# First routing search counted in PSUM ring banks, and the second expert's gather asked one block earlier

## The chip, the cores and the metric

The kernel is one program on one core of a Trainium2 chip. Its five engines run their own queues: TensorE (PE) with its weight loads (PEld), VectorE (DVE), ScalarE (ACT), GpSimd (POOL) and SyncE (SP), which mostly issues DMA transfers; POOL issues transfers too. The metric is the device time of one execution in microseconds, lower is better.

## The reference

Attention over 4 batches, 8 heads, 576 positions of 64 gives a matrix `x` of 2304 tokens by 512. Then a mixture of 8 experts and a feed-forward layer follow. What matters here is how tokens get their expert:

```
def _moe_ref(x, w_gate, w1, w2):
    ...
    cap = N // E                       # 2304 // 8 = 288
    logits = x @ w_gate
    order = np.argsort(-logits.flatten())
    assigned = -np.ones(N); counts = np.zeros(E)
    for idx in order:
        tok, e = idx // E, idx % E
        if assigned[tok] >= 0 or counts[e] >= cap:
            continue
        assigned[tok] = e
        counts[e] += 1
    for e in range(E):
        mask = assigned == e
        h = np.maximum(x[mask] @ w1[e], 0.0)
        out[mask] = h @ w2[e]

def _moe2_ref(x, w_in, w_out):
    h = x @ w_in
    g = np.maximum(h, 0.0) + np.log1p(np.exp(-np.abs(h)))
    return g @ w_out
```

## The kernel before

**Attention** fills the first 196 us, writes the tokens to a DRAM array `xs` and leaves the gate's logits `L` on chip, 18 columns of 128 tokens by 8 experts. Then `FFN.run` handles the experts one after the other in the order in which they fill up.

**Routing.** `Router.phase` finds one expert: the one that is full first, and its 288 tokens. It looks for the logit at which an expert's count reaches its capacity, by `search`: 4 steps over the high bits and 5 over the low ones, each a 32-way division. In a step DVE compares all keys with 31 thresholds, in two halves of 9 columns (line 601, into `rcmp`); PE counts per expert (two matmuls of line 610 with the capacities, 18 of line 614); DVE reduces the counts to the number of thresholds passed (line 617); PE spreads this number over the partitions (line 619); and DVE subtracts it from the keys (line 607) while the next step's comparisons have already read it. `r.key`, `r.lo`, the counts `r.pc`, the number `r.pn`, the tokens' positions `r.pos` and the index sums `r.pi` are all slices of one PSUM bank, tile `rt`. Between the steps DVE also converts pieces of the weight `w_in` (lines 527, 529, 532 on tiles `ce`), taken from the generator `load_in`.

After the search, DVE sums up who belongs to the expert (lines 654 to 689), PE turns this into positions (lines 692, 693), DVE compares the positions with a row of 128 numbers (line 711, three rounds of two, tiles `roa`), and PE sums the token numbers up (line 717). The result is `ridx` (line 725), by which `gather` fetches the tokens with three indirect DMAs from POOL (line 935, tiles `xr`). `Router.close` prepares the logits for the next expert. `route` strings the phases together as a generator: each `yield` gives a kind, the number of ticks to wait before the next piece, and a cost.

**One expert.** `xpose` transposes the gathered tokens on PE (line 949) and splits them into halves `xgh`, `xgl`. `H1` and `Y` are the expert's two layers, in 8 blocks. Then come 16 blocks `i` of the feed-forward layer: `H2(i + 2)` is a column block of `w_in` (12 matmuls, into a bank of the tag `ring`, which has 3 of them), `G` is the softplus on ACT and DVE (lines 995 to 1008, the last a copy of the remainder on POOL), and `O(i)` is the row block of `w_out` (6 matmuls of 512 columns into `acc`). In the first expert, `split_out` splits w_out's block into halves on ACT and POOL (line 917) and stores them to DRAM array `wh` (line 918, SP), and `load_out` loads them back for the next expert (line 925, POOL, 512 KB each). `tails` splits the last pieces of w_in (lines 858, 861).

**Who sets the order.** Each engine runs its instructions as the program is written; `run` writes it out by hand. Calls of `tick` between the blocks let one piece of routing into the stream when its wait is over; `until(e + 1)` writes out all that is left of the next expert's routing. For the first expert this stands behind block `U0 = 8`, together with the gather and `first_w`, which loads the next expert's first four weight blocks (SP, lines 883, 888). The blocks 10 to 13 each begin their `O` behind an `xpose` of the next expert.

Of the kernel before, what the change touches and what calls it, by code (L numbers as in the profile page):

```python
# [16 lines left out]
P = 128  # L17
# [3 lines left out]
E = 8  # L21
# [83 lines left out]
WARM2 = 26  # L105
EX = 1
AMPLE = (0.75, 1.0, 1.45)
U0 = 8
U1 = 7
LD = 0  # L110
PM = 20
# [425 lines left out]
class Router:  # L537


    def __init__(r, g, pool, work, bank):  # L540
        r.g, r.pool, r.work = g, pool, work
        nc = g.nc
        r.n = 0
        r.idxk = g.rcf[:, 0:18]
# [38 lines left out]

    def t(r, shape, dt, tag):
        r.n += 1
        bufs = 1 if tag in ("rown", "robw") else 8 if tag == "reid" else 2
        return r.work.tile(shape, dt, tag=tag, bufs=bufs, name=f"{tag}{r.n}")

    def open(r):
# [5 lines left out]
    def search(r, key, oh, scales):  # L595

        nc = r.g.nc
        pc, pn = r.pc, r.pn
        for n, i in enumerate(scales):
            for h, c in enumerate(((0, 9), (9, 18))):  # L600
                nc.vector.scalar_tensor_tensor(  # L601
                    r.cmp[:, h, 0 : 9 * 31].rearrange("p (c j) -> p c j", j=31), key[:, c[0] : c[1]].unsqueeze(2).to_broadcast([P, 9, 31]),
                    pn if n else 0.0, r.steps[i].unsqueeze(1).to_broadcast([P, 9, 31]),
                    op0=ALU.subtract, op1=ALU.is_ge,
                )
            if n:
                nc.vector.tensor_scalar(key, key, pn, None, op0=ALU.subtract)
            yield 2, 2, 1.0
            for p in range(2):
                nc.tensor.matmul(pc, r.row, r.kneg[:, p], start=p == 0, stop=False)  # L610

            for c in range(NCOL):
                cmp = r.cmp[:, c // 9, 31 * (c % 9) : 31 * (c % 9) + P]
                nc.tensor.matmul(pc, cmp, oh[:, c, :], start=False, stop=c == NCOL - 1)  # L614
            j = r.t([P, E], F32, "rjunk")
            full = r.t([P, 1], BF, "rge")
            nc.vector.tensor_scalar(j, pc, 0.0, None, op0=ALU.is_ge, op1=ALU.max, accum_out=full)
            yield 1, 1, 0.1
            nc.tensor.matmul(pn, r.pw[:, i, :], full, start=True, stop=True)  # L619
        nc.vector.tensor_scalar(key, key, pn, None, op0=ALU.subtract)  # L620

    def phase(r, last):
# [81 lines left out]
            )  # L704
        yield 0, 1, 1.1
        pi = r.pi
        for h in range(0, 6, 2):
            oa = []
            for c in range(3 * h, 3 * h + 6, 3):
# [39 lines left out]
class FFN:  # L749
    def __init__(f, g, I, out, ctx):  # L750
# [6 lines left out]
        f.ps = ps  # L757
        f.free = True
        f.n = 0
        f.r = Router(g, f.one, rw, f.bank("rt", 1))  # L760
        f.xg = [f.one.tile([P, 4, CAP], F32R, name=n) for n in ("xgh", "xgl")]
        f.yt = [f.one.tile([P, 4, CAP], F32R, name=n) for n in ("yth", "ytl")]

# [303 lines left out]
    def run(f):  # L1067
# [15 lines left out]
                    if e == 0:  # L1083
                        next(li, None)

        def tick(cost, go=True, near=False):

            nonlocal wait
            f.late = max(f.late + cost - HALF, -IDLE)
            wait -= 1  # L1090
            if wait <= 0 and go:
                _, wait, c = next(rt, (0, 999, 0.0))

                wait += 1 if near and c in AMPLE else 0
                f.late += c
            while f.late < LATE:
# [39 lines left out]
        for b in range(3):  # L1136
            for k in range(4):
                f.turn(ta[k], k, b)
        for k in range(4):
            f.xhalves(ta[k], k)  # L1140
        for _ in range(EX):
# [10 lines left out]
        for e in range(STOP):  # L1152
# [32 lines left out]
            for i in range(16):  # L1185
# [3 lines left out]
                    f.H2(e, i + 2)  # L1189
                elif more:  # L1190
                    f.H1(e + 1, i - 14)
                tick(0.0, i < 15)
                if i + 2 < 16:
                    f.split_out(e, i + 2)
                    f.G()
# [3 lines left out]
                if more and 10 <= i < 14:  # L1199
                    f.xpose(e + 1, i - 10)  # L1200
                f.O(e, i)
                if e and i < 8 or 8 <= i < 12:
                    f.load_out(16 * e + i + 8)
                if i < 15:
                    tick(1.0)
                if 1 <= i < 4 and f.done:
                    f.store()
                if more:
# [8 lines left out]
                    if b <= i:  # L1217
                        f.split_w(e + 1, 2, i - b)
                        f.load_w(e + 1, 2, i - b + 2)
            f.evac_o(e)  # L1220
        while f.done:
            f.store()
# [47 lines left out]
```

## Time and profile before

| | |
|---|---|
| median of 3 runs | 949.05 us (942.29 to 950.95) |
| the profiled execution | 946.9 us, span 945.1 us |
| PE busy | 854.9 us, 90% |
| DVE busy | 573.7 us, 61% |
| ACT busy | 474.1 us, 50% |
| POOL busy | 290.4 us, 31% |
| mean granted clock of PE | 0.951 |

The durations come from the one profiled execution; the span is the time in which its engines worked. Matmuls are pipelined, so that one row's duration is longer than the distance to the next matmul. A row in the timeline gives start, duration, engine, line, operation, what is written and read, the count, and in brackets how long its engine was idle before and who ended that. Line numbers are those of the kernel before.

### The profile page before, as it was taken

How to read it: one execution, taken by the hardware profiler on the slowest of the kernel's cores; microseconds unless marked ns; L12 is line 12 of the kernel's file. 1: busy time of each engine (PE TensorE's matmuls, PEld its weight loads, DVE VectorE, ACT ScalarE, POOL GpSimd, SP SyncE). 2: the span in 40 equal slices, each digit the busy share in tenths (PEclk: the TensorE clock that was granted, in tenths of full speed). 3: DMA queues.
4: the chain of work that ended last, by engine and by line, in shares of the span. 5: the costliest groups of instructions: out<-in, count | busy, mean ns of one | idle time of the engine just before them, and what ended most of it. 6: DMA issues, size and time to landing. Idle time of an engine off the chain costs nothing.

```text
span 945.1 us, 20697 instructions
## 1 busy us (share of the span) xinstructions
PE 854.9 (90%) x7732; PEld 763.5 (81%) x7732; DVE 573.7 (61%) x1642; ACT 474.1 (50%) x1187; POOL 290.4 (31%) x476
## 2 busy tenths in 40 slices
PE   7895887934999799999999999999999999999996
PEld 6674776833988689889888988898899889989985
DVE  5789764767976565675567555656764664344322
ACT  4674655521567444553455344435543563664442
POOL 7557331313876410320231023103300420330211
PEclk9899798966999899999999999999999999999999
DMA  9988687862435780765278156716760874585240
GB/s 246 248 251 261 172 245 216 247 204 83 133 114 201 239 265 23 226 193 164 60 233 251 41 160 171 217 36 189 200 207 20 239 226 143 140 230 170 86 115 34
DMA packets 98845, 163.07 MB, mean 173 GB/s; under 512 B 8841, under 2 KB 58553, under 8 KB 98745
## 3 DMA queue, kind: packets, MB, share of 16 engines
q1 hardware_dynamic: 73408, 88.03, 30.4%
q0 software_dynamic: 19104, 68.17, 24.9%
q10 hardware_dynamic: 6232, 5.56, 2.3%
q8 instruction: 61, 1.00, 0.4%
q14 instruction: 40, 0.32, 0.1%
HBM read 140.62 MB, written 21.10 MB: 171 GB/s over the span
## 4 chain that ended last, share of the span: by engine, by line
PE 58%; DVE 15%; DMA 12%; issue 6%; ACT 6%; POOL 2%; SPq 0%; ACTq 0%; DVEq 0%; POOLq 0%
PE acc L787 9%; PE ring L787 8%; PE ring L788 8%; PE ring L789 8%; PE acc L789 8%; PE acc L788 8%; DMA craw<-in_wout_dram 3%; DMA raw<-in_w_dram 3%; PE rt L614 2%; DMA vraw<-in_vr_dram 2%; DVE rcmp L601 2%; DMA xr<-xs,ridx 1%; DVE ce L529 1%; PE LG L382 1%; ACT hh L1005 1%
## 5 line engine op out<-in xcount | busy, mean ns | idle before, releaser
L1008 POOL CAST rem<-hh 128x64 fp32r<-128x64 f32 x128 | 31.4, 245 | 427.3 <-DVE hh L1006 427.2
L1004 DVE SCALAR_TENSOR_TENSOR ring<-ring,t 128x288 f32<-128x288 f32 x128 | 59.5, 465 | 102.9 <-ACT t L997 102.1
L787 PE MATMUL ring<-yth,wih 128*128 128x288 f32 x384 | 115.2, 300 | 0.0
L788 PE MATMUL ring<-ytl,wih 128*128 128x288 f32 x384 | 113.4, 295 | 0.0
L789 PE MATMUL ring<-yth,wil 128*128 128x288 f32 x384 | 113.0, 294 | 0.0
L787 PE MATMUL acc<-wo,hh 128*128 128x512 f32 x256 | 107.5, 420 | 0.0
L789 PE MATMUL acc<-wo,hh 128*128 128x512 f32 x256 | 101.9, 398 | 0.0
L788 PE MATMUL acc<-wo,hh 128*128 128x512 f32 x256 | 101.6, 397 | 0.0
L1006 DVE TENSOR_TENSOR hh<-ring,hh 128x288 fp32r<-128x288 f32 x128 | 58.6, 458 | 67.4 <-ACT hh L1005 66.4
L995 ACT ACTIVATE t<-ring 128x288 f32<-128x288 f32 x128 | 52.5, 410 | 87.2 <-PE ring L789 75.1
L1005 ACT ACTIVATE hh<-ring 128x288 fp32r<-128x288 f32 x128 | 52.7, 412 | 85.6 <-DVE ring L1004 84.9
L787 PE MATMUL ring<-xgh,w 128*128 128x288 f32 x256 | 78.5, 307 | 0.0
L789 PE MATMUL ring<-xgh,w 128*128 128x288 f32 x256 | 77.0, 301 | 1.4 <-POOL w L906 1.3
L788 PE MATMUL ring<-xgl,w 128*128 128x288 f32 x256 | 76.7, 300 | 0.0
L925 POOL DMA_DIRECT2D wo<-wh x112 | 60.4, 540 | 47.7 <-PE acc L789 28.0
L787 PEld LDWEIGHTS ring<-yth,wih 128*128 128x128 f32 x384 | 72.2, 188 | 2.4
L788 PEld LDWEIGHTS ring<-ytl,wih 128*128 128x128 f32 x384 | 72.2, 188 | 1.9
L900 ACT ACTIVATE w<-raw 128x512 fp32r<-128x512 f32 x95 | 58.2, 628 | 29.3 <-DMA raw<-in_w_dram 18.3
L789 PEld LDWEIGHTS ring<-yth,wil 128*128 128x128 f32 x384 | 72.2, 188 | 0.0
L965 ACT ACTIVATE hh<-ring 128x288 fp32r<-128x288 f32 x64 | 26.2, 410 | 80.9 <-PE ring L789 60.5
L903 DVE TENSOR_TENSOR w<-raw,w 128x512 fp32r<-128x512 f32 x79 | 53.6, 689 | 13.1 <-ACT w L900 13.0
L601 DVE SCALAR_TENSOR_TENSOR rcmp<-rt,rcf 128x279 bf16<-128x279 f32 x126 | 56.8, 494 | 4.2 <-PE rt L619 3.4
(217 smaller groups left out, 2308.9 us busy)
## 6 DMA issues: line engine op xcount, KB each, us to landing
wo<-wh POOLq DMA_DIRECT2D x112, 512.0 KB, 4.1
raw<-in_w_dram SPq DMA_DIRECT2D x128, 256.0 KB
craw<-in_wout_dram SPq DMA_DIRECT2D x16, 512.0 KB
wh<-wo SPq DMA_DIRECT2D x16, 512.0 KB
vz<-in_vp_dram ACTq DMA_DIRECT2D x36, 142.2 KB
vraw<-in_vr_dram SPq DMA_DIRECT2D x16, 288.0 KB
dnx<-dn SPq DMA_DIRECT2D x36, 128.0 KB
xs<-xl SPq DMA_DIRECT2D x36, 128.0 KB
```

The costliest lines, as they stand in the source:

```text
L601: nc.vector.scalar_tensor_tensor(r.cmp[:, h, 0 : 9 * 31].rearrange("p (c j) -> p c j", j=31), key[:, c[0] : c[1]].unsqueeze(2).to_broadcas ...
L787: nc.tensor.matmul(o, a[0], b[0], start=start, stop=False)
L788: nc.tensor.matmul(o, a[0], b[1], start=False, stop=False)
L789: nc.tensor.matmul(o, a[1], b[0], start=False, stop=stop)
L900: nc.scalar.activation(h[:, 0], raw, AF.Copy)
L903: nc.vector.tensor_tensor(h[:, 1], raw, h[:, 0].bitcast(F32), op=ALU.subtract)
L925: f.nc.gpsimd.dma_start(out=h, in_=f.g.wh[:, fb])
L995: nc.scalar.activation(t1, o, AF.Abs)
L1004: nc.vector.scalar_tensor_tensor(o, o, 0.0, t1, op0=ALU.max, op1=ALU.add)
L1005: nc.scalar.activation(h[:, 0], o, AF.Copy)
L1006: nc.vector.tensor_tensor(h[:, 1], o, h[:, 0].bitcast(F32), op=ALU.subtract)
L1008: nc.gpsimd.tensor_copy(f.rem[fb][:, :, c : c + 32], h[:, :, 2 * P : CAP])
```

## The change

Four things are edited.

- While the router has a `ring`, each search step takes its count `pc` and its number `pn` from a fresh bank of the tag `ring` in place of the slices of `rt`. The attribute is set to None behind the first expert's transpositions into `acc`; until then fall all nine steps of the first expert's search and the first step of the second's.
- In the same stretch, that is for the first expert alone, the positions are copied to an SBUF tile `rspos`, and the comparisons that build `roa` read this.
- `U0` becomes 7, and in the first expert's w_out blocks `tick` takes `soon`: a routing piece of kind 0 then waits for one tick instead of two.
- In the first expert's w_out blocks, `load_out` stands at the end of the block, behind `until`, the gather and the splits.

```diff
--- before.py
+++ after.py
@@ -105,7 +105,7 @@
 WARM2 = 26
 EX = 1
 AMPLE = (0.75, 1.0, 1.45)
-U0 = 8
+U0 = 7
 U1 = 7
 LD = 0
 PM = 20
@@ -537,8 +537,8 @@
 class Router:
 
 
-    def __init__(r, g, pool, work, bank):
-        r.g, r.pool, r.work = g, pool, work
+    def __init__(r, g, pool, work, bank, ring):
+        r.g, r.pool, r.work, r.ring = g, pool, work, ring
         nc = g.nc
         r.n = 0
         r.idxk = g.rcf[:, 0:18]
@@ -583,7 +583,7 @@
 
     def t(r, shape, dt, tag):
         r.n += 1
-        bufs = 1 if tag in ("rown", "robw") else 8 if tag == "reid" else 2
+        bufs = 1 if tag in ("rown", "robw", "rspos") else 8 if tag == "reid" else 2
         return r.work.tile(shape, dt, tag=tag, bufs=bufs, name=f"{tag}{r.n}")
 
     def open(r):
@@ -595,7 +595,7 @@
     def search(r, key, oh, scales):
 
         nc = r.g.nc
-        pc, pn = r.pc, r.pn
+        pn = None
         for n, i in enumerate(scales):
             for h, c in enumerate(((0, 9), (9, 18))):
                 nc.vector.scalar_tensor_tensor(
@@ -606,6 +606,7 @@
             if n:
                 nc.vector.tensor_scalar(key, key, pn, None, op0=ALU.subtract)
             yield 2, 2, 1.0
+            pc = r.ring()[:, 0:E] if r.ring else r.pc
             for p in range(2):
                 nc.tensor.matmul(pc, r.row, r.kneg[:, p], start=p == 0, stop=False)
 
@@ -616,6 +617,7 @@
             full = r.t([P, 1], BF, "rge")
             nc.vector.tensor_scalar(j, pc, 0.0, None, op0=ALU.is_ge, op1=ALU.max, accum_out=full)
             yield 1, 1, 0.1
+            pn = r.ring()[:, 0:1] if r.ring else r.pn
             nc.tensor.matmul(pn, r.pw[:, i, :], full, start=True, stop=True)
         nc.vector.tensor_scalar(key, key, pn, None, op0=ALU.subtract)
 
@@ -704,6 +706,9 @@
             )
         yield 0, 1, 1.1
         pi = r.pi
+        if r.ring:
+            pos = r.t([P, NCOL], F32, "rspos")
+            nc.vector.tensor_copy(pos, r.pos.bitcast(I32))
         for h in range(0, 6, 2):
             oa = []
             for c in range(3 * h, 3 * h + 6, 3):
@@ -757,7 +762,7 @@
         f.ps = ps
         f.free = True
         f.n = 0
-        f.r = Router(g, f.one, rw, f.bank("rt", 1))
+        f.r = Router(g, f.one, rw, f.bank("rt", 1), f.bank)
         f.xg = [f.one.tile([P, 4, CAP], F32R, name=n) for n in ("xgh", "xgl")]
         f.yt = [f.one.tile([P, 4, CAP], F32R, name=n) for n in ("yth", "ytl")]
 
@@ -1083,14 +1088,15 @@
                     if e == 0:
                         next(li, None)
 
-        def tick(cost, go=True, near=False):
+        def tick(cost, go=True, near=False, soon=False):
 
             nonlocal wait
             f.late = max(f.late + cost - HALF, -IDLE)
             wait -= 1
             if wait <= 0 and go:
-                _, wait, c = next(rt, (0, 999, 0.0))
-
+                kind, wait, c = next(rt, (0, 999, 0.0))
+
+                wait = 1 if soon and kind == 0 and wait < 999 else wait
                 wait += 1 if near and c in AMPLE else 0
                 f.late += c
             while f.late < LATE:
@@ -1136,6 +1142,7 @@
         for b in range(3):
             for k in range(4):
                 f.turn(ta[k], k, b)
+        f.r.ring = None
         for k in range(4):
             f.xhalves(ta[k], k)
         for _ in range(EX):
@@ -1189,7 +1196,7 @@
                     f.H2(e, i + 2)
                 elif more:
                     f.H1(e + 1, i - 14)
-                tick(0.0, i < 15)
+                tick(0.0, i < 15, False, e == 0)
                 if i + 2 < 16:
                     f.split_out(e, i + 2)
                     f.G()
@@ -1199,10 +1206,10 @@
                 if more and 10 <= i < 14:
                     f.xpose(e + 1, i - 10)
                 f.O(e, i)
-                if e and i < 8 or 8 <= i < 12:
+                if e and i < 12:
                     f.load_out(16 * e + i + 8)
                 if i < 15:
-                    tick(1.0)
+                    tick(1.0, True, False, e == 0)
                 if 1 <= i < 4 and f.done:
                     f.store()
                 if more:
@@ -1217,6 +1224,8 @@
                     if b <= i:
                         f.split_w(e + 1, 2, i - b)
                         f.load_w(e + 1, 2, i - b + 2)
+                if e == 0 and 8 <= i < 12:
+                    f.load_out(i + 8)
             f.evac_o(e)
         while f.done:
             f.store()
```

Behind the edits line numbers move: 610 becomes 611, 614 becomes 615, 617 becomes 618, 619 becomes 621, 689 and 692 become 691 and 694, 711 becomes 716, 717 becomes 722, 723 becomes 728, 743 becomes 748, 1004 and 1006 become 1009 and 1011.

PE, the end of one search step and the start of the next (`rt` is the one bank, `ring` a ring bank, `rge` the reduced counts); before:

```order
L619 LDWEIGHTS rpw [waits Pool_49]
L619 MATMUL rt_2941<-rge_3052,rpw 128x1 [waits DVE_49]
L610 LDWEIGHTS rrow
L610 MATMUL rt_2941<-rkneg,rrow 128x8 [waits DVE_49]
L610 LDWEIGHTS rrow
L610 MATMUL rt_2941<-rkneg,rrow 128x8
L614 LDWEIGHTS rcmp
L614 MATMUL rt_2941<-roh_3023,rcmp 128x8
```

and now, one step later:

```order
L621 LDWEIGHTS rpw
L621 MATMUL ring_3089<-rge_3084,rpw 128x1 [waits DVE_49]
L611 LDWEIGHTS rrow
L611 MATMUL ring_3096<-rkneg,rrow 128x8
L611 LDWEIGHTS rrow
L611 MATMUL ring_3096<-rkneg,rrow 128x8
L615 LDWEIGHTS rcmp [waits DVE_49]
L615 MATMUL ring_3096<-roh_3023,rcmp 128x8
```

The wait for DVE has moved from the first matmul of a count, behind which all others queue, to the first weight load from the comparisons; the tenth of the eighteen loads has a second one, for the second half.

DVE, the first expert's w_out blocks with the second expert's positions (`roa`), index (`ridx`), and the blocks' G (`ring` and `hh`; hh_4465 before and hh_4507 now are of H2(8), ring_4531 is H2(10)); before:

```order
L1006 TENSOR_TENSOR hh_4465<-ring_4443,hh_4465 128x288
L861 TENSOR_TENSOR wll_4324<-xr_4326,wlh_4323 128x512
L711 TENSOR_TENSOR roa_4484<-rt_2941,rcf 128x384
L711 TENSOR_TENSOR roa_4486<-rt_2941,rcf 128x384
L1004 SCALAR_TENSOR_TENSOR ring_4488<-ring_4488,t_134_4501 128x288
L1006 TENSOR_TENSOR hh_4510<-ring_4488,hh_4510 128x288
L711 TENSOR_TENSOR roa_4527<-rt_2941,rcf 128x384
L711 TENSOR_TENSOR roa_4529<-rt_2941,rcf 128x384
L1004 SCALAR_TENSOR_TENSOR ring_4531<-ring_4531,t_139_4544 128x288
L1006 TENSOR_TENSOR hh_4553<-ring_4531,hh_4553 128x288
L723 COPY riv_4572<-rt_2941 128x3
L725 SCALAR_TENSOR_TENSOR ridx_4574<-rt_2941,riv_4572 128x3
```

and now:

```order
L1009 SCALAR_TENSOR_TENSOR ring_4426<-ring_4426,t_144_4439 128x288
L1011 TENSOR_TENSOR hh_4452<-ring_4426,hh_4452 128x288
L866 TENSOR_TENSOR wll_4346<-xr_4286,wlh_4345 128x512
L716 TENSOR_TENSOR roa_4471<-rt_2941,rcf 128x384
L716 TENSOR_TENSOR roa_4473<-rt_2941,rcf 128x384
L716 TENSOR_TENSOR roa_4499<-rt_2941,rcf 128x384
L716 TENSOR_TENSOR roa_4501<-rt_2941,rcf 128x384
L1009 SCALAR_TENSOR_TENSOR ring_4475<-ring_4475,t_149_4488 128x288
L1011 TENSOR_TENSOR hh_4507<-ring_4475,hh_4507 128x288
L866 TENSOR_TENSOR wll_4346<-xr_4348,wlh_4345 128x512
L728 COPY riv_4526<-rt_2941 128x3
L730 SCALAR_TENSOR_TENSOR ridx_4528<-rt_2941,riv_4526 128x3
```

The second and third round of comparisons follow each other directly, and the index stands two blocks earlier, behind G(8) instead of G(10).

POOL, the second gather (`xr`) among the weight halves of w_out (`wo` from `wres`), remainders (`rem`) and the load for the next expert (`wo` from `wh`); before:

```order
L917 TENSOR_TENSOR wo_4549<-wres_76,wo_4549 128x512
L1008 COPY rem_2977<-hh_4553 128x2x32
L925 DMA wo_4564<-wh 128x1024
L935 DMA xr_4576<-xs,ridx_4574 128x512
L935 DMA xr_4578<-xs,ridx_4574 128x512
L935 DMA xr_4580<-xs,ridx_4574 32x512
L917 TENSOR_TENSOR wo_4630<-wres_76,wo_4630 128x512
```

and now:

```order
L922 TENSOR_TENSOR wo_4561<-wres_75,wo_4561 128x512
L1013 COPY rem_2976<-hh_4565 128x2x32
L940 DMA xr_4585<-xs,ridx_4528 128x512
L940 DMA xr_4587<-xs,ridx_4528 128x512
L940 DMA xr_4589<-xs,ridx_4528 32x512
L922 TENSOR_TENSOR wo_4632<-wres_76,wo_4632 128x512
L1013 COPY rem_2977<-hh_4636 128x2x32
L930 DMA wo_4649<-wh 128x1024
```

The gather has moved ahead of one weight half, one remainder and the load; its three DMAs stand in one piece in both. On SP, the loading of the expert's number and its first four weight loads (lines 883, 888) likewise stand ahead of one store of `wh` that was ahead of them.

## Rows read from the trace of the kernel before

**Rows 1.** Busy time by stage: PE, PEld, DVE, ACT, POOL, granted clock, DMA share, GB/s.

```profile
196.00:228.00 32.00, 9.03 (x212) 7.78 (x212) 25.17 (x99) 5.94 (x15) 3.19 (x5) 0.50 0.41 141
...
245.00:271.00 26.00, 23.25 (x223) 22.25 (x223) 24.88 (x54) 13.38 (x31) 23.36 (x30) 0.94 0.37 113
...
312.00:319.50 7.50, 1.15 (x4) 0.60 (x4) 3.73 (x14) 2.16 (x6) 5.07 (x8) 0.75 1.05 338
319.50:323.00 3.50, 3.50 (x12) 2.92 (x12) 1.17 (x3) 0.41 (x1) 0.00 (x0) 0.56 1.08 411
```

**Rows 2.** Timeline of one search step, DVE and PE.

```profile
201.95 0.17 DVE L617 TENSOR_SCALAR_CACHE_REDUCE rjunk<-rt 128x8 f32<-128x8 f32 x1 [0.44 <-PE rt L614]
...
202.38 0.94 DVE L601 SCALAR_TENSOR_TENSOR rcmp<-rt,rcf 128x279 bf16<-128x279 f32 x2
203.35 0.25 DVE L607 TENSOR_SCALAR rt<-rt 128x18 f32<-128x18 f32 x1
203.51 0.42 DVE L529 SCALAR_TENSOR_TENSOR ce<-wo,ce 128x256 int32<-128x256 int32 x1
203.65 0.19 PE L610 MATMUL rt<-rkneg,rrow 128*128 128x8 bf16 x2 [1.31 <-DVE rt L607]
...
204.36 0.17 DVE L617 TENSOR_SCALAR_CACHE_REDUCE rjunk<-rt 128x8 f32<-128x8 f32 x1 [0.44 <-PE rt L614]
```

**Rows 3.** Timeline, the first step of the second search.

```profile
207.91 0.81 DVE L601 SCALAR_TENSOR_TENSOR rcmp<-rt,rcf 128x279 bf16<-128x279 f32 x2
...
209.48 0.17 DVE L617 TENSOR_SCALAR_CACHE_REDUCE rjunk<-rt 128x8 f32<-128x8 f32 x1 [0.43 <-PE rt L614]
```

**Rows 4.** The chain of waits, positions and index (start, us, what).

```profile
223.67 0.94 DVE roa L711 x2
...
227.81 0.17 DVE riv L723
```

**Rows 5.** Tile xr, the first expert's gather: DMA from issue to landing.

```profile
DMA to landing us min/median/max: 2.8/3.7/4.2
```

**Rows 6.** Timeline of DVE, the second expert's routing in the w_out blocks.

```profile
294.12 0.17 DVE L689 TENSOR_SCALAR rgot<-rt 128x18 f32<-128x18 f32 x1
...
308.40 0.15 DVE L723 COPY riv<-rt 128x3 f32<-128x3 f32 x1
...
311.09 0.45 DVE L1004 SCALAR_TENSOR_TENSOR ring<-ring,t 128x288 f32<-128x288 f32 x1
...
312.45 0.30 DVE L628 TENSOR_REDUCE rm<-rt 128x18 f32<-128x144 f32 x1
...
315.12 0.18 DVE L646 SCALAR_TENSOR_TENSOR rt<-rt,rcf 128x18 f32<-128x18 int32 x1
```

**Rows 7.** Timeline of PE, from H2(7) to H2(13).

```profile
293.51 0.30 PE L787 MATMUL ring<-yth,wih 128*128 128x288 f32 x1
...
300.37 0.29 PE L717 MATMUL rt<-robw,roa 128*128 128x6 bf16 x6 [0.59 <-DVE roa L711]
...
308.66 0.39 PE L787 MATMUL acc<-wo,hh 128*128 128x512 f32 x1
...
310.05 0.29 PE L787 MATMUL ring<-yth,wlh 128*128 128x288 f32 x1
...
316.21 0.45 PE L949 MATMUL ring<-identf,xr 128*128 128x128 f32 x1 [4.40 <-DMA xr<-xs,ridx]
318.80 0.72 PE L949 MATMUL ring<-identf,xr 128*128 128x128 f32 x2 [2.15 <-DMA xr<-xs,ridx]
319.45 0.80 PE L787 MATMUL acc<-wo,hh 128*128 128x512 f32 x1
...
322.18 0.44 PE L787 MATMUL ring<-yth,wlh 128*128 128x288 f32 x1
```

**Rows 8.** Tile xr, the second gather: POOL's issues (min/median/max ns), DMA to landing.

```profile
L935 POOL DMA_INDIRECT xr<-xs,ridx x3: 867/952/1031, 309.9 to 312.5; - x3
...
DMA to landing us min/median/max: 6.2/6.4/7.5
```

## The prediction

> **What bounds the kernel now.** I read the busy time by stage first [rows 1]. TensorE (PE) is the bound nearly everywhere after 323 us; two places are not PE-bound, and the change touches both. From 196 to 228 us PE is busy 9.03 of 32 us while VectorE (DVE) is busy 25.17: this is the first expert's search, a ping-pong between two engines, and nothing of the experts can start before it. From 312 to 319.5 us PE is busy 1.15 of 7.5 us: it waits for the second expert's tokens. Between 245 and 271 us DVE, at 24.88 of 26, is the tighter engine; its work there comes in a fixed order behind the search, so that stage moves with the search as a block.
>
> Then the timeline of one search step [rows 2]. DVE's reduction L617 stands at 201.95, the pair of comparisons L601 from 202.38 to 203.32, the subtraction L607 from 203.35 to 203.60. Only then does PE start counting, with L610 at 203.65, after 1.31 us idle that is put down to L607; 20 small matmuls later, at 204.36, DVE, which has waited 0.44 us for PE, has its next L617. A step takes 2.41 us.
>
> Last, the second gather, on three engines [rows 6 to 8]. GpSimd (POOL) issues a 512 KB weight load and right behind it the three gathers, between 309.9 and 312.5 [rows 8]; they land 6.2 to 7.5 us after their issue, against 2.8 to 4.2 for the first expert's [rows 5]. PE waits 4.40 and then 2.15 us for them at the first transposition, and the O block behind it runs slowly [rows 7].
>
> **The change part by part. Search.** Nothing is removed. Today every count waits for both comparisons and, in all but the first step of a search, for L607, since counts and keys lie in one bank. In the new order the first nine counts wait for the first comparison and the last nine for the second; L607 drops out of the chain. Today L617 comes 1.04 us after the pair's end (203.32 to 204.36 [rows 2]). The 20 matmuls take 0.71 of it, so nine take some 0.32; with 0.05 for the hand-over (203.60 to 203.65) and as much for the last one's way, PE would let the reduction (now L618) start 0.43 after the pair. But DVE still has L607 and one conversion (L529, 0.42 us, starting 0.19 after the pair) to do there, so that L618 can start some 0.55 after the pair. The step then takes 1.93 us, and DVE, not PE, sets it. Saved: 0.48 us in each of 7 steps, 3.4 us. In the 2 first steps, which have no L607, L617 comes 1.57 us after L601 [rows 3] and would come at 0.81 + 0.43 = 1.24: 0.3 each, 0.6. Bounds for the search: 2.6 (conversions late, 0.35 and 0.1 a step) to 4.3 (0.55 and 0.25).
>
> **Positions.** Three pairs of L711 run from 223.67, L723 starts at 227.81 [rows 4]: 4.14 us, of which the pairs are some 3 (0.94 for the first in the chain), and the rest is waiting for PE behind each pair, since the positions share the bank that PE writes. The copy costs as much as another 18-column operation on this tile, 0.17 us (L689) [rows 6]. With the positions elsewhere the six comparisons can follow each other at about 0.5 us, and only the last three matmuls remain behind: 0.22 + 3.05 + 0.35 = 3.6. Saved 0.5, between 0.2 and 0.7. [...] No row here shows that comparison from SBUF.
>
> The second expert's first search step also gets a ring bank: 0.3 us on the chain to the first transpositions. The first gather needs 2.8 to 4.2 us to land and is asked as much earlier as the search ends [rows 5], so it doesn't take over. Search, positions and this step: **4.8 us**, between 3.1 and 5.4. All later queues start behind the first routing, so the gain should arrive at 245 us whole.
>
> **Second gather.** I walked the queues of the new order on the clock of the old trace. Moved earlier by about two blocks: the positions' matmuls, the index and the closing of expert 1's routing. A block is one H2 (12 matmuls, 1.59 us) and one O (1.39 us, 308.66 to 310.05 [rows 7]). What the crowding costs PE, each from 0 to the figure:
> (a) L694 now stands straight behind O(4), at 293.51, and needs rgot, which ends at 294.29 [rows 6]: 0.8.
> (b) The first pair of comparisons ends about 297.6 and PE is there at 297.4: 0.2.
> (c) The second half of the index matmuls stands right behind H2(8), at 299.4; its comparisons stand behind G(7) and half of a weight split on DVE and end near 300.85 by my walk: 1.5. Today's wait of this kind is 0.59 [rows 7].
> (d) DVE's closing of the routing, 2.69 us (308.40 to 311.09), now stands ahead of G(9), and the 2.8 us of L628 to L646 ahead of G(10) [rows 6]. So G(9) ends near 308.5, and the gather, which on POOL stands behind this block's remainder copy, starts at 308.8, not at 309.90: hardly one microsecond earlier, though it is asked a whole block earlier. And the third expert's first counts, which now stand between O(9) and H2(12), wait for comparisons that end at 313.3 while PE is there at 311.6: 1.7.
> PE then comes to the first transposition at 315.7, where it came at 311.8 before. The third gather goes out at 311.4 and lands between 314.2 (2.8 us) and 318.9 (7.5): the 512 KB load is no longer ahead of it, but the four weight loads on SyncE's queue (SP) move up with it. I take 4.9 us, 316.3, between the two rows. O(10) then starts at 316.7, against 319.45: 2.75. To this comes 0.75 us of the third expert's counts, which are done by then. [...] Sum **4.2 us** (2.75 + 0.75 + 1.34 - 0.67), from 0 (all waits, gather as slow as now) to 8.7 (no wait at all).
>
> The DMA share is 1.05 while the gather is out [rows 1]. [...]
>
> The POOL queue: the three gathers, 1.3 us apart, are moved past one weight subtraction, its copy and the store behind it; the block that reads this weight comes after the transpositions, which cover it. The load that moved behind the splits is needed one expert later: nothing.
>
> **Sum.** The profiled execution took 946.9 us (span 945.1 and 1.8 around it); 4.8 + 4.2 = 9.0 gives 937.9. It lies 2.15 below the median of the three runs shown, so on the median's scale: 949.05 - 9.0 = **940.0 us**.
>
> **The rivals.** First: DVE keeps up, the waits (a) to (d) don't appear, and the gather lands before PE is there. The idle 6.55 us, the rest of the transposition and the slow clock all go, 8.7: with the search 13.5, 935.5 us. For it: the one wait for the index comparisons in today's trace is 0.59; against it, DVE's 2.69 and 2.8 us runs now stand ahead of the blocks' own work. Second: the wait is only moved, the transition gives nothing and the search its 4.8: 944.2 us. For it: the gather starts one microsecond earlier by my walk, with DMA saturated. Third: DVE is slower in a step than I read (conversions wait on ScalarE), 0.2 a step; with positions and the transition 1.9 + 4.2: 943. Fourth, slower: each of the three long new waits (a, c, d) is followed by a stretch at the lower clock like that after 316, in which O(10) lost 1.34 and the block as a whole about 3.4 us; 3 x 3.4 and waits of 4.2 against the 8.7 that go make the transition 5.7 worse, 0.9 beyond the search's gain: 950. It decides from about three such stretches. Against it: after the wait at 300.37 the blocks ran on at full speed, O(9) in 1.39.
>
> **How the numbers follow.** Forecast (gain 6 to 11.5) 0.49; first rival 0.2; second 0.19; third 0.08; slower 0.04. Range 932.5 to 947: the first rival with the upper search bound and 1 us for the spread, and the second with the lower bound; it leaves out the slower case and both tails. Runs of one kernel lie 0.9% apart (942.29 to 950.95), so about 1%, 9.5 us, is what can be told from no change. Faster by over 1% needs a gain above 9.5: all of the first rival and two fifths of the forecast, 0.41; slower by over 1% 0.02; the rest within.
>
> **What would show it.** In the search, L611 starts right behind the previous matmul, L618 shows little or no wait for PE, and steps come every 1.9 us; if they come at 2.2, the third rival. The first gather stands near 223.9, H1 near 232.5. In the transition: L722 with a wait near 1.5 us, L611 near 1.7, the second gather near 304 (308.8 less the search's gain), and PE's wait on the transposition below 1 us; a wait of 3 us or more is the second rival, no waits at all the first. I am wrong altogether if the stage from 245 us doesn't move with the search.

## The result, and the profile after

| | kernel before | changed kernel |
|---|---|---|
| median, us | 948.35 (4 runs, 942.29 to 950.95) | 935.16 (4 runs, 933.32 to 936.55) |
| profiled execution / its span, us | 946.9 / 945.1 | 936.42 / 934.7 |

The ratio is 0.9863, 95% interval 0.9824 to 0.9902: 13.2 us less between the medians (9.3 to 16.7). The forecast was 9.0; the profiled pair shows 10.5. A second measurement, below, gave 0.9899 (0.9852 to 0.9947), 9.6 us by the ratio.

The search first. The timeline of the changed kernel, DVE and PE, one step (start, us, engine, line, what; in brackets the idle time before it and who ended it); it answers to [rows 2]:

```profile
201.63 0.16 DVE L618 TENSOR_SCALAR_CACHE_REDUCE rjunk<-ring 128x8 f32<-128x8 f32 x1
...
201.87 0.20 PE L611 MATMUL ring<-rkneg,rrow 128*128 128x8 bf16 x2
202.05 0.94 DVE L601 SCALAR_TENSOR_TENSOR rcmp<-rt,ring,rcf 128x279 bf16<-128x279 f32 x2
...
202.62 0.83 PE L615 MATMUL ring<-roh,rcmp 128*128 128x8 bf16 x18 [0.55 <-DVE rcmp L601]
203.02 0.25 DVE L607 TENSOR_SCALAR rt<-rt,ring 128x18 f32<-128x18 f32 x1
203.18 0.42 DVE L529 SCALAR_TENSOR_TENSOR ce<-wo,ce 128x256 int32<-128x256 int32 x1
203.51 0.16 DVE L618 TENSOR_SCALAR_CACHE_REDUCE rjunk<-ring 128x8 f32<-128x8 f32 x1
```

L618 to L618 takes 1.88 us, where it took 2.41. L611 stands behind the previous matmul, the counts L615 start after the first comparison and not after L607, and L618 no longer waits for PE: DVE has no gap from 201.63 to 203.51. The positions, on DVE, answering to [rows 4]:

```profile
219.87 0.17 DVE L711 CAST rspos<-rt 128x18 f32<-128x18 int32 x1
220.07 2.90 DVE L716 TENSOR_TENSOR roa<-rspos,rcf 128x384 bf16<-128x384 f32 x6
223.31 0.16 DVE L728 COPY riv<-rt 128x3 f32<-128x3 f32 x1 [0.34 <-PE rt L722]
```

Six comparisons in a row and one wait of 0.34 behind them. The transition, on PE (with one row of DVE), answering to [rows 7]:

```profile
289.42 0.17 PE L694 MATMUL rt<-rsel,rcb 128*128 128x18 bf16 x1 [0.66 <-DVE rgot L691]
...
296.12 0.29 PE L722 MATMUL rt<-robw,roa 128*128 128x6 bf16 x6 [1.46 <-DVE roa L716]
...
307.70 0.80 DVE L601 SCALAR_TENSOR_TENSOR rcmp<-rt,rcf 128x279 bf16<-128x279 f32 x2
...
308.55 0.19 PE L611 MATMUL rt<-rkneg,rrow 128*128 128x8 bf16 x2 [1.44 <-issue]
...
310.76 0.31 PE L954 MATMUL ring<-identf,xr 128*128 128x128 f32 x1
312.27 0.50 PE L954 MATMUL ring<-identf,xr 128*128 128x128 f32 x2 [1.20 <-DMA xr<-xs,ridx]
312.70 0.50 PE L792 MATMUL acc<-wo,hh 128*128 128x512 f32 x1
...
314.19 0.30 PE L792 MATMUL ring<-yth,wlh 128*128 128x288 f32 x1
```

The waits of 4.40 and 2.15 us for the gather have shrunk to 1.20; three others, at L694, L722 and L611, have come. The one at L611 ends with the comparisons L601, 307.70 to 308.50, though the profile puts it down to "issue". The 1.20 is a wait for the second of the three gathers: the third was there when PE came to it, since the row of two transpositions has no gap. O(10), 312.70 to 314.19, takes 1.49 us where it took 2.73. POOL's issues, answering to [rows 8]:

```profile
304.43 1.00 POOL L940 DMA_INDIRECT xr<-xs,ridx  x1 [0.48 <-POOL rem L1013]
305.74 0.94 POOL L940 DMA_INDIRECT xr<-xs,ridx  x1 [0.31 <-PE ring L794]
306.99 0.87 POOL L940 DMA_INDIRECT xr<-xs,ridx  x1 [0.30 <-issue]
```

The gather is still held by the remainder copy, as the walk had it. Busy time by stage (PE, PEld, DVE, ACT, POOL, granted clock, DMA share, GB/s), answering to [rows 1]:

```profile
196.00:228.00 32.00, 15.72 (x232) 11.77 (x233) 29.04 (x121) 7.40 (x17) 6.78 (x12) 0.53 0.49 158
...
307.50:312.50 5.00, 2.75 (x35) 2.40 (x34) 3.38 (x11) 3.43 (x9) 4.37 (x7) 1.00 0.99 333
312.50:316.00 3.50, 3.50 (x27) 3.10 (x27) 1.10 (x3) 1.02 (x3) 1.97 (x3) 1.00 1.06 386
```

The granted clock behind the transposition is 1.00, where it was 0.56.

**Where the time went, by stages.** The profiled executions differ before the change reaches them: the first comparison of the search, behind the same attention part, stood between 192.46 and 201.01 us in the 14 profiles of this study, and at 197.97 in the kernel before. So I count from the first comparison to the first O block, O(0), and from O(0) on; all numbers are starts in the timelines, in us. "H1" in the table is the first H1 behind the second gather, so the second expert's. The expectations below call it the third expert's, which is a slip; the counts at L611 are the third expert's.

| kernel | search to O(0) | O(0) to: second gather | O(10) | second expert's H1 | O(15) | from O(15) to the last O |
|---|---|---|---|---|---|---|
| before | 79.85 | 32.08 | 41.63 | 56.58 | 61.86 | 595.5 |
| changed | 74.49 | 31.52 | 39.79 | 53.41 | 58.89 | 593.0 |
| e0_both | 74.49 | 31.53 | 39.15 | 52.76 | 58.25 | 594.4 |
| e1_search | 74.59 | 32.06 | 41.65 | 56.63 | 61.91 | 596.7 |
| e2_transition | 78.69 | 31.57 | 39.24 | 52.86 | 58.34 | 594.9 |
| e3_rings | 75.20 | 32.07 | 41.27 | 56.28 | 61.56 | 595.0 |
| e5_load_only | 75.62 | 31.48 | 41.51 | 56.62 | 61.89 | 593.6 |
| e7_block6, e7b | 75.38, 75.60 | 27.75 | 38.41 | 52.0 | 57.5 | 596.2, 594.6 |
| e11_counts_one_later | 74.54 | 27.74 | 36.69 | 50.34 | 55.62 | 595.4 |
| e8_early_steps_block8 | 75.05 | 35.32 | 44.41 | 60.58 | 66.07 | 596.9 |
| e6_no_soon | 75.76 | 29.85 | 38.21 | 53.14 | 58.64 | 609.8 |
| e9_hold | 74.63 | 30.53 | 39.46 | 55.82 | 60.60 | 610.5 |
| e10_block6_hold | 75.67 | 27.76 | 36.15 | 50.96 | 55.74 | 617.2 |

Up to O(0) the kernels with the search part differ by up to 1.3. In four profiles (e5, both of block 6, e10) the first expert's twelve transpositions take 1.1 longer (a median of 417 to 421 ns each in place of 272): the granted clock there is 0.54 in e5 and 1.00 in the changed kernel. With a ring 4 of 12 profiles show this, and 2 more a smaller part of it, without a ring none of 2, so whether it is scatter or a cost of the change is not shown. e2, without the search part, stands 1.16 ahead of the kernel before at O(0) although all instructions up to there are the same: from 60 to 74 us after the first comparison its granted clock is 1.00, that of the kernel before 0.88. A difference of about 1 us up to O(0) therefore says nothing by itself.

### The profile page after: what moved, and what is told of

Read it like the earlier page. It is cut to its first block, busy times and chain, and to the rows that moved or that the text cites. A ratio compares the mean times of both kernels' runs of the same rounds, so it can differ in the third digit from the quotient of the medians.

```text
span 934.7 us, 20697 instructions
## 1 busy us (share of the span) xinstructions
PE 854.6 (91%) x7732; PEld 763.0 (82%) x7732; DVE 570.6 (61%) x1643; ACT 473.1 (51%) x1187; POOL 288.8 (31%) x476
## 4 chain that ended last, share of the span: by engine, by line
PE 62%; DVE 12%; DMA 10%; issue 6%; ACT 5%; POOL 4%; SPq 1%; POOLq 0%; ACTq 0%
PE acc L792 10%; PE ring L792 9%; PE ring L793 9%; PE acc L794 8%; PE acc L793 8%; PE ring L794 8%; DMA vraw<-in_vr_dram 3%; PE rt L615 2%; DMA craw<-in_win_dram 1%; DMA xr<-xs,ridx 1%; PE ring L954 1%; DVE rcmp L601 1%; DVE ce L529 1%; ACT hh L1010 1%; DVE ring L1009 1%
## 5 line engine op out<-in xcount | busy, mean ns | idle before, releaser
L1002 ACT ACTIVATE t<-t 128x288 f32<-128x288 f32 x128 | 56.9, 445 | 4.1
```

What stands on the lines that cost most here:

```text
L1002: nc.scalar.activation(t1, t2, AF.Ln, bias=1.0)
```

## The experiments

**The parts, and the whole again.** Four kernels on one chip. Edits are shown against the changed kernel; those of e3 and e5 against e1, that of e10 against e9.

e0_both: no edit. 

> The changed kernel itself, repeated, so that the parts can be set against it on one chip. Theory (the parts add up in their stages): 10.4 us below the kernel before, as in the profiled pair (search 5.4, transition 3.2, the rest after it), ratio 0.989. First rival (the transition is worth 8 or more): 13.2 us, ratio 0.986, as the medians of the first runs have it.

Measured: 936.05 us, ratio 0.9899 (0.9852 to 0.9947). By stages 5.4 in the search and 3.8 up to the second expert's H1: the theory. The medians are 11.1 apart, the ratio makes 9.6, and its interval holds 13.2 as well, so the times alone don't decide.

e1_search: the search part alone.

```diff
-U0 = 7
+U0 = 8
-tick(0.0, i < 15, False, e == 0)
+tick(0.0, i < 15)
-tick(1.0, True, False, e == 0)
+tick(1.0)
-if e and i < 12:
+if e and i < 8 or 8 <= i < 12:
     f.load_out(16 * e + i + 8)
...
-if e == 0 and 8 <= i < 12:
-    f.load_out(i + 8)
```

> Search and positions alone; the second gather as before. Theory: first matmul of the first expert's H1 near 232.1 when the search starts at 198.0 (5.2 earlier), the wait at the second expert's first transposition is still over 4 us and the gain is 5.2, ratio 0.9945. Rival (only the whole change gains in the transition because the waits of the two parts are tied): the earlier block runs into a gather that is no faster, and less than 3 us is left at the end, ratio 0.997 or more.

Measured: 0.9921 (0.9891 to 0.9951). The gain of 5.3 at O(0) is still 5.2 at O(15). The waits at the transposition stay at 4.34 and 2.25 us. The stages move as a block; the rival falls. PE at the second expert's transposition:

```profile
308.61 0.45 PE L954 MATMUL ring<-identf,xr 128*128 128x128 f32 x1 [4.34 <-DMA xr<-xs,ridx]
311.31 0.72 PE L954 MATMUL ring<-identf,xr 128*128 128x128 f32 x2 [2.25 <-DMA xr<-xs,ridx]
```

e2_transition: the second gather's part alone.

```diff
-f.bank("rt", 1), f.bank)
+f.bank("rt", 1), None)
```

> The second gather's part alone; search and positions as before. Theory: the search steps come every 2.4 us again; from the first O block on, 3.2 us are gained up to the third expert's first H1, and some 2 more behind it, since the routing of all later experts stands at other places; 5.2 in sum, ratio 0.9945. Rival (what comes behind the transition is one clock drop that the kernel before had at 400 to 420 us): 3.2 in the transition and, against a run of before without such a drop, nothing more; ratio 0.9965. Second rival (first rival of the prediction): 8 us, ratio 0.9915.

Measured: 0.9938 (0.9907 to 0.997). O(0) to the second expert's H1 is 3.7 shorter, and the waits are the same as with the whole change (1.47 at L722, 1.43 at L611, 0.60 at the transposition). By stages the parts add up, 5.3 and 3.7 against 5.4 and 3.8 for the whole; by times they make 7.5 and 5.9 against 9.6, which the intervals allow. From O(15) on the orders of before (before, e1, e3, e5: 593.6 to 596.7) and of the change (changed, e0, e2: 593.0 to 594.9) overlap: the 2 us that I expected there aren't shown.

e3_rings: e1 without the copy of the positions.

```diff
-        if r.ring:
+        if 0:
             pos = r.t([P, NCOL], F32, "rspos")
```

> Ring banks in the search alone; positions read from the shared bank as before, second gather as before. Theory: all of the search part but 0.5 us of the positions: 4.7 us, ratio 0.995; six position comparisons take some 4.1 us from the first to the index again. [...]

Measured: 0.9933 (0.9897 to 0.997). From the first comparison to the index's copy `riv` it is 29.84 in the kernel before, 25.66 here and 24.87 with the positions: the rings give 4.18, the positions 0.79. Why 0.79, the groups of DVE in e1_search show (count | busy us, mean ns of one | idle before):

```profile
L716 DVE TENSOR_TENSOR roa<-rt,rcf 128x384 bf16<-128x384 int32 x42 | 21.4, 550 | 4.9 <-PE rt L722 4.3
...
L716 DVE TENSOR_TENSOR roa<-rspos,rcf 128x384 bf16<-128x384 f32 x6 | 2.9, 552 | 0.0
```

The later experts' comparisons still read PSUM: 550 ns, against 552 from SBUF, so the comparisons themselves are no shorter. What goes is the two waits of 0.39 us between the pairs (e3_rings still has them) and a little of each of six comparisons now in one row, 2.90 against three pairs of 1.01; the copy takes 0.20 back.

**What makes the gather late.**

e5_load_only: e1 with the weight load moved behind the gather.

```diff
-if e and i < 8 or 8 <= i < 12:
+if e and i < 12:
     f.load_out(16 * e + i + 8)
...
+if e == 0 and 8 <= i < 12:
+    f.load_out(i + 8)
```

> Search part, and of the transition only the weight load moved behind the gather; gather at block 8 as before, routing steps as before. Counted from the first comparison of the search, the third expert's first H1 stood at 136.4 in the kernel before, 131.2 with the search part alone and 127.3 to 127.9 with the whole change. Theory (the load ahead in GpSimd's queue is what slowed the gather): gathers go out 0.6 earlier and land in about 5 us, the two waits at the transposition fall from 6.6 to about 4, H1 at 128.9. Rival (SP's loads saturate the DMA engines, the load ahead costs only its issue): 130.6.

Measured: 0.9946 (0.9909 to 0.9982), 56.62 to the second expert's H1, no gain. POOL and PE in this kernel:

```profile
305.94 0.87 POOL L940 DMA_INDIRECT xr<-xs,ridx  x1 [0.30 <-issue]
306.81 0.62 POOL L930 DMA_DIRECT2D wo<-wh  x1
...
308.91 0.30 PE L954 MATMUL ring<-identf,xr 128*128 128x128 f32 x1 [2.99 <-DVE rt L645]
311.02 0.48 PE L954 MATMUL ring<-identf,xr 128*128 128x128 f32 x1 [1.82 <-DMA xr<-xs,ridx]
313.17 0.31 PE L954 MATMUL ring<-identf,xr 32*128 32x32 f32 x1 [1.67 <-DMA xr<-xs,ridx]
```

Three waits, 6.48 us in sum, against 6.59 in e1; the first is put down to DVE, but the transposition needs nothing of that line, so it was the gather too. From issue to use the three gathers took 5.5, 6.3 and 7.2 us. In e1, with the load ahead, they took 6.3 and 7.6, and the third at most 7.1. So the first two came sooner and the last did not, and the last ended the wait: the load ahead alone is not what makes the transposition late, and my theory of it falls. Here the load goes out right behind the third gather (306.81), in the changed kernel only 2.3 us after the third's issue. That a load close behind slows the last gather is a rival which no run here separates.

e8_early_steps_block8: the change with its gather, and the next expert's first weight loads with it, one block later.

```diff
-U0 = 7
+U0 = 8
```

> The whole change, with early routing steps, but the gather asked at block 8; TensorE's and VectorE's orders are those of the changed kernel. Counted from the first O block: theory (the place of the gather in GpSimd's queue decides): the gather goes out about 2 later than with the change, PE waits about 3 at the first transposition in place of 1.2 and may lose clock behind it: 55 to 56. Rival (SP's loads set when the gather lands, whenever it is asked): 53.4, as with the change.

Measured: 0.9985 (0.9949 to 1.0022), and 60.58, worse than the kernel before in this stage by 4.0. The rival falls. PE:

```profile
308.85 0.19 PE L611 MATMUL rt<-rkneg,rrow 128*128 128x8 bf16 x2 [1.44 <-DVE rcmp L601]
...
309.88 0.44 PE L792 MATMUL ring<-yth,wlh 128*128 128x288 f32 x1
...
314.90 0.47 PE L954 MATMUL ring<-identf,xr 128*128 128x128 f32 x1 [2.63 <-DMA xr<-xs,ridx]
316.98 0.71 PE L954 MATMUL ring<-identf,xr 128*128 128x128 f32 x2 [1.61 <-DMA xr<-xs,ridx]
317.62 0.80 PE L792 MATMUL acc<-wo,hh 128*128 128x512 f32 x1
318.22 0.63 PE L793 MATMUL acc<-wo,hh 128*128 128x512 f32 x1
```

Here all the waits stand one behind the other, the old and the new. The granted clock falls before the waits for the gather: behind L611, with the same wait of 1.44 as in the changed kernel, H2(12) starts at full speed and from 309.88 takes 0.44 us a matmul in place of 0.29. O(10) then takes 0.63 a matmul in place of 0.39. The granted clock is 0.50 in each of these stretches:

```profile
309.90:312.00 2.10, 2.10 (x10) 1.99 (x9) 0.62 (x3) 0.00 (x0) 1.80 (x3) 0.50 1.00 282
312.00:317.00 5.00, 0.76 (x5) 0.35 (x3) 2.11 (x5) 2.23 (x5) 4.52 (x7) 0.50 1.08 351
317.00:320.00 3.00, 3.00 (x8) 2.23 (x9) 0.46 (x1) 0.41 (x1) 0.00 (x0) 0.50 1.05 397
320.00:323.00 3.00, 3.00 (x14) 2.90 (x12) 0.00 (x0) 0.00 (x0) 0.00 (x0) 0.50 0.47 175
```

Between block 8 and block 7 lie 7.2 to 7.8 us, more than I expected. The gather itself goes out 3.8 later than with the change and O(10) starts 4.6 to 5.3 later; the rest of the 7.2 to 7.8 comes behind O(10)'s start, where the clock is the lower one. The next expert's first weight loads moved with the gather, so the two are not separated. The gathers took 6.4 and 7.1 us to their use, though no load of POOL's was ahead of them.

e7_block6:

```diff
-U0 = 7
+U0 = 6
```

> The whole change with the gather asked at block 6 in place of 7: the index is there at the end of block 6, but the gather stands behind the next block's remainder copy on GpSimd, and that behind VectorE's closing. Counted from the first comparison: theory: gather at 101.6 in place of 106.0, the wait of 1.2 at the transposition goes, the one of 1.44 at the third expert's counts stays, H1 of the third expert at 126.4 (127.3 to 127.9 with the change). Rival: the weight subtraction behind the gathers on GpSimd, 1.7 later, makes PE wait as long at the O block: 127.6 or later.

e7b_block6_again: the same kernel. 

> Gather at block 6, repeated to time it better against the kernel before. Theory: 52.0 from the first O block to the third expert's first H1 again, 0.7 to 1.4 less than with the change; ratio 0.988, not told apart from the change's own 0.986 and 0.990 by the times alone. Rival (what it gains is lost again in later stages, as the first run's end suggested): stage as in the theory, but the end no better than the changed kernel's 726.4 to 727.1 from the first comparison.

Measured: 0.9886 (0.9839 to 0.9933) and 0.9898 (0.9854 to 0.9942). The gather goes out 3.8 us earlier against O(0) and has landed when PE comes; of the waits behind O(9) only L611's is left:

```profile
309.63 0.19 PE L611 MATMUL rt<-rkneg,rrow 128*128 128x8 bf16 x2 [1.45 <-DVE rcmp L601]
...
311.85 0.59 PE L954 MATMUL ring<-identf,xr 128*128 128x128 f32 x3
```

In the stage this is 0.8 to 1.4 us better, as expected. At the end (729.1 and 727.7 from the first comparison to the last O, 726.4 and 727.1 with the change) nothing of it is seen; a gain of this size is within what later stages scatter.

**The routing steps.**

e6_no_soon: the gather at block 7, without the early steps.

```diff
-tick(0.0, i < 15, False, e == 0)
+tick(0.0, i < 15)
-tick(1.0, True, False, e == 0)
+tick(1.0)
```

> The whole change without its early routing steps: gather asked at block 7, but the position steps come every second place as before, so that what is left of them stands in one row at the end of block 7. Counted from the first O block of the first expert, the third expert's first H1 stood at 56.6 in the kernel before and with the search part alone, at 52.8 to 53.4 with the whole change and at 52.0 with the gather at block 6. Theory (the steps of the routing have to be spread over the blocks before): PE waits about 2 more for the comparisons in a row than with the change, and the gather goes out about 1 later; 54.5 to 55.5. Rival (asking at block 7 is all that counts, the early steps are not needed): 53.4 or less.

Measured: slower, 1.009 (1.0055 to 1.0125). In the transition the rival holds: 53.14, as good as the change, in spite of a wait of 2.34 us at L722; the gather went out 1.7 us earlier than with the change, not 1 later. But from O(15) on 609.8, 13 to 17 more than the kernels above it in the table. PE, two of the waits that come behind it:

```profile
300.50 0.29 PE L722 MATMUL rt<-robw,roa 128*128 128x6 bf16 x6 [2.34 <-DVE roa L716]
...
428.22 0.40 PE L792 MATMUL acc<-hh,wo 128*128 128x288 f32 x1 [0.96 <-DVE xr L1033]
...
460.86 0.17 PE L664 MATMUL rt<-rac,rcb 128*128 128x8 bf16 x1 [1.19 <-DVE rac L661]
```

PE's waits over 0.3 us behind 330 us add up to 19.1 in this kernel and to 7.1 in the changed one. Nothing makes up for steps that come late here, so all later experts have their routing steps at other places among the blocks. That the added waits are the cause of the longer stages is argued from these sums.

e9_hold:

```diff
-tick(0.0, i < 15, False, e == 0)
+tick(0.0, i < 15 and not (e == 0 and i == 7), False, e == 0)
-tick(1.0, True, False, e == 0)
+tick(1.0, not (e == 0 and i == 7), False, e == 0)
```

> The whole change, but the two routing steps of block 7 (the closing of expert 1's routing and the next key) come two steps later, so that VectorE has the blocks' own work first; gather at block 7. Counted from the first comparison: theory (my step d: the closing on VectorE holds up the remainder copy and with it the gather): gather at 103.7 in place of 106.0, no wait at the transposition, none at the third expert's counts, H1 at 125.0. Rival (the gather is bound by the DMA engines, not by its issue): it lands no earlier and PE waits at the transposition what it no longer waits at the counts, H1 at 127 or later.

Measured: slower, 1.0101 (1.0064 to 1.0139). POOL and PE:

```profile
303.89 1.29 POOL L922 TENSOR_TENSOR wo<-wres,wo 128x512 fp32r<-128x512 f32 x1 [2.05 <-ACT wo L921]
...
312.63 0.33 PE L954 MATMUL ring<-identf,xr 128*128 128x128 f32 x1 [1.68 <-DMA xr<-xs,ridx]
314.26 0.31 PE L954 MATMUL ring<-identf,xr 32*128 32x32 f32 x1 [1.30 <-DMA xr<-xs,ridx]
```

The gather goes out 1.0 earlier and not 2.3: now it is behind a weight half that waits 2.05 us for ScalarE. The wait at L611 is gone, and PE waits 1.68 and 1.30 for the gathers instead, as the rival had it. O(10) falls to matmuls of 0.63 us and takes 2.73, and the later stages take 14 to 18 more.

e10_block6_hold: e9, and the gather at block 6.

```diff
-U0 = 7
+U0 = 6
```

> Both: gather asked at block 6, and the routing steps of block 7 two steps later. Counted from the first comparison: theory: gather at 101.6, no wait at the transposition or the counts, H1 of the third expert at 125.0, the same as with the later steps alone since the gather is no longer last. Rival: GpSimd's late weight subtraction costs 1 to 2: 126 to 127.

Measured: slower, 1.0053 (1.0032 to 1.0073). O(0) to the second expert's H1 is 50.96, near the theory (125.0 is 50.5 by this count); a wait of 0.52 is left at L611. The later stages take 20 to 24 more. e9 and e10 have the same order on TensorE, and e6 has it too from within the third expert's search on; all three lose there.

e11_counts_one_later:

```diff
-U0 = 7
+U0 = 6
-tick(1.0, True, False, e == 0)
+tick(1.0, not (e == 0 and i == 9), False, e == 0)
...
+owed = 1
...
+if e == 1 and i > 1 and owed and wait == 2:
+    wait, owed = 1, 0
 tick(0.4, i < 7, e > 1)
```

> Gather at block 6, and of the third expert's first counts the place alone: one routing step is held back once, so that they stand behind the next H2 block, and made up for in the second expert's first product, so that all later experts have the order of the changed kernel. Counted from the first O block: theory: the wait of 1.44 at the counts goes and nothing takes its place; 50.6 (52.0 with the gather at block 6), and the later experts lose nothing, since the order is made up for (with the steps two later for good they lost 2 to 7 each). Rival: the later steps of this expert wait instead, 52.0.

Measured: 935.59 us, 0.987 (0.9813 to 0.9928). PE:

```profile
308.04 0.20 PE L611 MATMUL rt<-rkneg,rrow 128*128 128x8 bf16 x2
...
308.55 0.59 PE L954 MATMUL ring<-identf,xr 128*128 128x128 f32 x3
```

Neither waits any more; the waits at L694 and L722 are still there. The stage is 50.34, 2.4 to 3.1 less than with the change, and from O(15) on 595.4, no longer than in the kernels with the order of before or of the change: the step that was made up costs nothing later. From the first comparison to the last O it is the shortest, 725.5 against 726.4 and 727.1; by its time it isn't told apart from the changed kernel.

## Why the prediction was right

**Search: right, and the term holds.** Predicted were 4.0 us for the rings, and e3_rings measured 4.18; a step was to take 1.93 us and takes 1.88, and it is DVE that sets it, not PE. The second expert's first step was to give 0.3 and gave 0.25: from the first comparison to the first transposition it is 32.23 against 37.43, and 4.95 of that is there at `riv`. The third rival (steps of 2.2) falls by this. H1 was expected near 232.5 and stands at 232.54, but in an execution whose search began 0.45 later; counted from the search the gain is 5.2 and not 4.8.

**Positions: mis-sized, 0.5 (0.2 to 0.7) for 0.79.** The stretch takes 3.4 and not 3.6 (copy to `riv`, 219.87 to 223.31), and was 4.2 before. The comparisons are not shorter from SBUF (552 ns, against 550 from PSUM, both in e1_search); the six in one row take 2.90 us, where the prediction had 3.05.

**Arrives whole at 245 us: right.** The gain is 5.2 at H1 and 5.4 at O(0), and e0 and e1 agree (5.4 and 5.3). Against e2, whose granted clock was higher ahead of O(0), it would be 4.2.

**Transition: right in kind, in part by luck: 4.2 forecast, 3.2 (changed), 3.8 (e0) and 3.7 (e2) measured.** The new waits came nearly as worked out: (a) 0.8, measured 0.66; (b) 0.2, none; (c) 1.5, measured 1.46; (d) 1.7 at L611, measured 1.44. The sum can be redone from the rows. PE's waits were 0.59 and 6.55 before, 7.1 us; they are 0.66, 1.46, 1.44 and 1.20 now, 4.8. That is 2.4 less. O(10) at the full clock gives 1.24, and one more count of the third expert (308.55 to 309.05) now stands ahead of O(10) and takes 0.5. Together 3.1, against 3.2 measured.

In the prediction's own terms three sizes were off. O(10) was to start 2.75 us earlier and started 1.84 earlier (2.48 in e0). The third expert's counts, 0.75, gave nothing up to H1: one step is done sooner, but the next takes its place, so that two counts lie between O(10) and H1 in both kernels. And the 0.67 taken off the 1.34 was not lost. The last two nearly cancel, which is luck. The 1.34 is what O(10) took more than O(9) before, 2.73 us against 1.39 [rows 7]; with the granted clock at 1.00 O(10) took 1.49, and 1.24 was gained. The 0.67, half of the 1.34, was the author's estimate for a fall of the clock behind one of the new waits, and no run shows that term: in the changed kernel the clock was 1.00 from 287 to 316 us, behind all of these waits, and in e8, where it fell to 0.50, O(10) took the whole 2.73.

The gather was to land 4.9 us after its issue, and the third was to end the wait. It was the second: 6.5 us from issue to use in the changed kernel and 5.9 in e0 and e2, against 7.6 before. It starts 0.56 us earlier against O(0), where the prediction had 1.1. The reason given for the quicker landing, the load ahead, is not borne out: e5 moved the load away and gained nothing, and in e8, with no load of POOL's ahead, the second gather took 7.1. In e5 the last one took 7.2 us, at a DMA share of 1.06 from its issue to its use; the first expert's gather in the kernel before took 2.8 to 4.2 [rows 5], at a share of 0.40 from its first issue to its use (228.5 to 235.4). That the other traffic sets it is argued from this, not shown; the cause of the quicker landing stays open.

**The rivals.** The first, 13.5, has the number of the first measurement and not its mechanism: the waits (a), (c) and (d) are there and PE still waits for the gather. Stage sums are 5.4 and 3.2 to 3.8, 8.5 to 9.2 against a forecast of 9.0; what lies behind is some 1 us on the mean (594.1 for three profiles with the order of the change, 595.2 for four with that of before) and not separated from scatter. The second falls by e2. The fourth, a new wait followed by the lower clock, did not happen in the changed kernel, e0, e2 or the two of block 6, and did happen in e8 behind the same wait of 1.44 at L611. So the prediction was right to price it; it came once in six profiles.

**The range.** Its lower end, 932.5, does not follow from its working: 949.05 less 5.4, 8.7 and 1 is 933.95. The measured 935.16 lies inside either.

**What the prediction didn't price:** the change moves the routing steps of all later experts. In this order the stages behind O(15) are not longer, though PE's waits over 0.3 us there add up to 7.1 to 7.5 in the three profiles with the order of the change and to 4.9 to 5.8 in the four with that of before. In the order of e6, e9 and e10 it cost 13 to 24 us, more than the whole gain.

## What to carry to other kernels

Where two engines take turns on one tile (here all slices of one PSUM bank), the wait chain of one step shows what a second bank can give: read off it, 4.0 us were predicted for the nine steps, and e3_rings measured 4.18. Where work is dealt out step by step among blocks, a step moved once shifts everything behind it. Look at the last stages, not only at the one that was edited, and make the step up soon: e11 did, and its later stages are no longer than before. When runs scatter by more than the gain, count from an event that the change doesn't reach. The times told 9.6 from 13.2 us no better than within 4; the stages repeat to 0.7 us from O(0) to H1, and to 1.3 up to O(0).

## What was not expected of the hardware

Behind the same attention part, with the same instructions, the search began anywhere from 192.46 to 201.01 us in different executions. In the two kernels that were profiled twice this start differs by 6.0 and 2.7 us, and the whole time by 4.8 and 4.0. TensorE held its full clock behind waits of 1.44 and 1.20 us in the changed kernel (granted clock 1.00, O(10) in 1.49). In e8, behind the same wait of 1.44, the granted clock fell to 0.50 from 309.9 us on, while TensorE was busy, and O(10) took 2.73. A comparison over 128x384 took 550 ns with its positions in PSUM and 552 ns with them in SBUF.
